# Engine programs in the main block without a closing barrier, and a small input loaded behind ScalarE's table load

## The chip, the cores and the metric

The kernel runs on one core of one Trainium2 chip. The metric is the device time of one execution in microseconds (us), and 2% (4.3 us) is what counts as faster or slower. There is also the *span* of a profiled execution: the time from its first to its last instruction in the trace. The time is longer than the span, and the difference, "time minus span" below, holds what the runtime does around the kernel and the trace does not show. Engines are called PE (TensorE), DVE (VectorE), ACT (ScalarE), POOL (GpSimd) and SP (SyncE); an added q, as in SPq, is that engine's sequencer.

## The reference, cut to what matters

```python
xn = _layernorm(A_x)                                   # A_x: (4, 1, 576)
out = A_x + A(xn, k_cache, v_cache, wq, wo) + B(xn, w1, w2, w3, w4)
# A: q = xn @ wq; attention over the last 2048 cached positions, 16 KV heads, batch 4; @ wo
# B: layernorm, gelu(@ w1), shifted, @ w2, add, layernorm, gelu(@ w3) @ w4, add
```

One token per batch entry: hardly any arithmetic and 88.5 MB of weights and cache to read. The input x has 4.5 KB.

## The kernel before

A helper collects each engine's operations in a list, sorts it by a key, resolves the waits to semaphore counts and emits the list as that engine's program. SP issues nearly all transfers, in one long queue. The parts that the change touches:

```python
# x on ACT's queue, first thing; the large wq load heads SP's queue
ev_x = add_dma([(x_sb[:], x2)], "x", (), -100, engine="act")
ev_wq = [add_dma([(kt_t[:], A_wq[0:512, :].rearrange("(p r) n -> p (r n)", r=4))], "wq", (), -60), ...]
...
# the end: two copies out of PSUM, two stores, each engine waits for its own store to land
for h, eng in ((0, "sp"), (1, "act")):
    ev_o[h] = add_dma([(o2[:, HALF * h:HALF * (h + 1)], out_sb[32 * h:32 * h + B, ...])], ("out", h),
                      [f"fin{h}"], 10000, engine=eng)
    add(eng, lambda e: None, [ev_o[h]], None, 10001)
...
# five programs in a Block: each engine jumps to its own block, then to a common end block
with nc.Block() as block:
    @block.sync
    def _(e):
        emit_program("sp", e)
    ...                                    # gpsimd, vector, scalar, tensor alike
```

When the `Block` is left, every engine branches to an end block in which a barrier stands: each of the four other engines drains and reports to POOL, POOL waits for the four reports and releases all. An equal barrier, which the program's constructor puts there, opens the kernel; the change leaves that one alone.

Of the kernel before, what the change touches and what calls it, by code (L numbers as in the profile page):

```python
# [8 lines left out]
ACTF = mybir.ActivationFunctionType  # L9
# [26 lines left out]
def bass_parallel_sum__sliding_block_cached__mixer_s_mlp__decode_kernel(  # L36
    nc, A_x, A_k_cache, A_v_cache, A_wq, A_wo, B_x, B_w1, B_w2, B_w3, B_w4, out
):
    B, Sq, D = A_x.shape
    _, Hkv, Sk, Dh = A_k_cache.shape  # L40
    Hq = A_wq.shape[1] // Dh
    F = B_w3.shape[1]
# [14 lines left out]
    x2 = A_x.rearrange("b s d -> (b s) d")  # L57
    o2 = out.rearrange("b s d -> (b s) d")

    with ExitStack() as ctx:  # L60
        def sb(name, shape, dt):
            return ctx.enter_context(nc.sbuf_tensor(name, shape, dt))

        def sem(name):
            return ctx.enter_context(nc.semaphore(name))
# [26 lines left out]
        x_sb = sb("x_sb", [B, D], BF16)  # L92
# [18 lines left out]
        act_dummy = sb("act_dummy", [1, 2], BF16)  # L111
# [9 lines left out]
        zeros_bf = sb("zeros_bf", [128, 512], BF16)  # L121
# [35 lines left out]
        def add(engine, emit, waits=(), sig=None, key=0.0, inc=(), loop=None, cond=None):  # L157
            seqc[0] += 1
            prog[engine].append(Op(emit, waits, sig, key, seqc[0], inc, loop, cond))

        def tok(nm):
            if nm not in S:
                S[nm] = sem("t_" + "_".join(str(k) for k in (nm if isinstance(nm, tuple) else (nm,))))
            return nm
# [6 lines left out]
        def add_dma(pairs, skey, waits=(), key=0.0, engine="sp"):  # L171
            tok(skey)
            dma_count[skey] = dma_count.get(skey, 0) + 16 * len(pairs)

            def emit(e):
                for o_, i_ in pairs:
                    e.dma_start(o_, i_).then_inc(S[skey], 16)  # L177
            add(engine, emit, waits, None, key)
            return ("dma", skey, dma_count[skey])
# [11 lines left out]
        def pool_ident(t, tag, pattern, view, key):  # L191
# [19 lines left out]
            waits=["ident_f"], sig="mU", key=-8)  # L211
# [1 line left out]
            add("dve", lambda e, x=x: e.tensor_copy(out=mU_bf[:, :, x], in_=mU[:]), waits=["mU"], sig=f"mU_bf{x}", key=-7.8)  # L213


        ev_x = add_dma([(x_sb[:], x2)], "x", (), -100, engine="act")
        ev_wq = [add_dma([(kt_t[:], A_wq[0:512, :].rearrange("(p r) n -> p (r n)", r=4))], "wq", (), -60),
                 add_dma([(wqrag, rag_src(A_wq))], "wqr", (), -59)]
        ev_w2 = add_dma([(w2main, B_w2[0:512, :].rearrange("(p r) n -> p r n", r=4)), (w2rag, rag_src(B_w2))], "w2", (), -58)
# [98 lines left out]
        for b in range(B):  # L318
            add("dve", lambda e, b=b: e.tensor_copy(out=qp_out[:, b], in_=qp_in[:, b]), waits=["qTp", "qpad_zero"],
                sig="qT" if b == B - 1 else None, key=-29.4)  # L320
# [3 lines left out]
        def pe_zero(e):  # L324
# [2 lines left out]
                ins = e.matmul(Sps[:, q, :], lhsT=zeros_bf[:, 0:128], rhs=zeros_bf[:, :], start=True, stop=True)  # L327
            return ins
        add("pe", pe_zero, waits=["zeros_bf", "perm_bf", "gelu_h", "x1", "xnT"], sig=None, key=-7.5)
        add("act", lambda e: e.activation(out=act_dummy[:], in_=zeros_bf[0:1, 0:2], func=ACTF.Copy), waits=["zeros_bf"], inc=[(tok("evA"), 1)], key=-0.5)  # L330
        add("dve", lambda e: e.tensor_copy(out=dve_dummy[:], in_=zeros_bf[0:1, 0:2]), waits=["zeros_bf"], inc=[(tok("evD"), 1)], key=-0.5)

# [29 lines left out]
        for c in range(NC):  # L362
            lp = ("K", c // NPOS)
            for k in range(NBLK):
# [6 lines left out]
                    key=NBLK * c + k + 0.2)  # L371
# [4 lines left out]
              waits=["qT", "qs_zero"] + ([f"SC{c - NPOS}"] if c >= NPOS - 1 else []), inc=[("qs", 1)], key=c)  # L376
# [6 lines left out]
            waits=["rmax"], sig="negb", key=KS + 0.05)  # L383
        for q in range(4):
            add("act", lambda e, q=q: e.activation(out=P_sb[:, q, :], in_=Sps[:, q, :], func=ACTF.Exp,
                                                   bias=negb[:, 0:1], scale=scale, accum_out=rs4[:, q:q + 1]),
                waits=["negb"], sig=f"exp{q}", key=KS + 0.1 + 0.01 * q)

        for q in range(4):
# [3 lines left out]
                waits=[f"PTx{q}", "permT_bf"] + (["PT0"] if q == 3 else []), sig=f"PTy{q}", key=k0)  # L393
            add("act", lambda e, q=q: e.activation(out=PT_t[:, 512 * q:512 * (q + 1)], in_=ps[:, 4 + q % 3, :], func=ACTF.Copy),
                waits=[f"PTy{q}"], sig=f"PT{q}", key=k0 + 0.16)
# [3 lines left out]
            waits=["rinv", "ident_f"], sig="diag", key=KS + 0.82)  # L399
        add("pe", lambda e: e.matmul(rinvps, lhsT=ones_f[:], rhs=diag[:], start=True, stop=True), waits=["diag", "ones_f", "exp3"],  # L400
            sig="rinvp", key=KS + 0.9)
        add("dve", lambda e: e.tensor_copy(out=rinvB[:].rearrange("p (c u e) -> p c u e", u=NU, e=2),
                                           in_=rinvps.rearrange("p (u c e) -> p c u e", u=NU, e=2)),
            waits=["rinvp"], sig="rinvB", key=KS + 1.5)
# [20 lines left out]
        for c in range(NC):  # L425
# [4 lines left out]
                key=KV + 2 * c, loop=("V", gq))  # L430
            if b == B - 1:
                hv = lambda t, gq=gq: t[:, 0:128].rearrange("p (b h) -> p b h", b=B)[:, :, 8 * gq:8 * gq + 8]
                add("dve", lambda e, hv=hv: e.tensor_tensor(out=hv(OTn), in0=OTps.rearrange("p (b h) -> p b h", b=B), in1=hv(rinvB), op=ALU.mult),  # L433
                    waits=["rinvB", f"PV{c}"], sig=f"OTn{gq}" if gq == 3 else None, inc=[(tok("otn"), 1)] if gq < 3 else [], key=KV + 2 * c + 0.1)
# [13 lines left out]
        def pe_AO(half):  # L448
# [10 lines left out]
            waits=["OTy"], sig="ORp", key=KT - 2.5)  # L459
# [30 lines left out]
        for h in range(2):  # L490
# [3 lines left out]
                waits=[f"hs{h}", "ln1"], sig="x1" if h else "x1a", key=-29 + 0.6 * h)  # L494
# [4 lines left out]
        for h in range(2):  # L499
            add("act", lambda e, h=h: e.activation(out=h_sb[:, HALF * h:HALF * (h + 1)], in_=HTps[h], func=ACTF.Gelu_apprx_tanh),  # L500
                waits=[f"hT{h}", "x1nT"], sig="gelu_h" if h else None, key=-20 + 0.1 * h)
# [29 lines left out]
        for k in range(3):  # L531
            add("act", lambda e, k=k: e.activation(out=h2g[:, 384 * k:384 * (k + 1)], in_=H2ps[k], func=ACTF.Gelu_apprx_tanh), waits=["h2_3"],
                sig="gelu2" if k == 2 else None, key=-0.9 + 0.1 * k)

        def pe_h2T(e):
# [7 lines left out]
            waits=["h2T"], inc=[("evA", 1)], key=-0.3)  # L543
        add("dve", lambda e: e.tensor_copy(out=h2o[:, :, 8, :], in_=H2Tb.rearrange("p (g y) -> p g y", g=4)[..., 0:B]),  # L544
            waits=["h2T"], inc=[("evD", 1)], key=-0.3)
# [35 lines left out]
        def emit_op(eng_name, engine, op, waited):  # L581
            for w in op.waits:
                if isinstance(w, tuple) and w[0] == "take":
                    engine.wait_ge(S[w[1]], w[2]).then_inc(S[w[1]], -w[2])  # L584
                    continue
                s_, v_ = resolve(w)
                if waited.get(s_.num, 0) >= v_:
                    continue
                waited[s_.num] = v_
                engine.wait_ge(s_, v_)  # L590
            ins = op.emit(engine)
            if op.sig is not None:
                ins.then_inc(S[eng_name], 1)
            for nm, n in op.inc:
                ins.then_inc(S[nm], n)

        def emit_program(eng_name, engine):
            waited = {}
            ops = prog[eng_name]
            if eng_name == "pe":  # L600
                hop = engine.alloc_register("hop")
                engine.reg_mov(hop, 0)
            i = 0
            while i < len(ops):
                if ops[i].loop is None:
                    emit_op(eng_name, engine, ops[i], waited)
                    i += 1
                    continue
                name = ops[i].loop[0]
                passes = {}  # L610
                while i < len(ops) and ops[i].loop is not None and ops[i].loop[0] == name:
                    passes.setdefault(ops[i].loop[1], []).append(ops[i])
                    i += 1
                shape = [[(op.sig is None, [w[1:] for w in op.waits], op.inc) for op in p] for p in passes.values()]
                assert all(x == shape[0] for x in shape) and list(passes) == list(range(len(passes)))
                assert all(w[0] == "take" for p in passes.values() for op in p for w in op.waits)
                with engine.bass.Fori(0, len(passes), engines=OrderedEngineSet([engine.engine]), head_slot={engine.engine: 0}):
                    inner = nc.cur_bb
                    for k, op in enumerate(passes[0]):
                        emit_op(eng_name, engine, op, waited)  # L620
                        if (name, k) in HOPS:
                            engine.br_eq(hop, 0, on_true=f"hop_{name}", on_false=f"fall_{name}")
                            nc.switch_bb(f"fall_{name}", parent=inner)
                            engine.sem_inc(S["hop"], 1)
                            engine.br(f"hop_{name}")
                            nc.switch_bb(f"hop_{name}", parent=inner)

        with nc.Block() as block:
            @block.sync
            def _(e):  # L630
                emit_program("sp", e)

            @block.gpsimd
            def _(e):
                emit_program("pool", e)

            @block.vector
            def _(e):
                emit_program("dve", e)

            @block.scalar
            def _(e):
                emit_program("act", e)

            @block.tensor
            def _(e):
                emit_program("pe", e)


# [26 lines left out]
```

## Time and profile before

| | before |
|---|---|
| time, median of 3 runs (range) | 215.94 us (215.93 to 216.82) |
| span of the profiled execution | 214.09 us |
| time minus span, same execution | 1.81 us |
| packets of weights and cache: first starts, last ends | 1.85 us, 211.10 us |

From the page of the kernel before: the busy share of the 16 DMA engines in 40 equal slices of the span, in tenths, and SP's queue with packets, MB and share of 16 engines' span.

```profile
DMA  7999999999999999999999999999999999999992
...
q1 hardware_dynamic: 7432, 88.50, 97.7%
```

The transfers never pause, so they are the bound; only what lies before the first and after the last packet can be saved. The chain of waits of the kernel before, its last pieces (start us, us, what):

```profile
179.19 31.22 DMA w<-in_B_w_dram
210.41 0.04 issue
210.46 1.39 PE ps L438 x18
211.85 0.44 DVE out_sb L560
```

The head, from the timeline of the kernel before (start us, us, engine line operation, out<-in, count, and in brackets the idle time in front and what ended it):

```profile
0.81 0.42 SPq L177 DMA_DIRECT2D kt<-in_A_wq_dram  x1
0.82 0.56 ACTq L177 DMA_DIRECT2D x_sb<-in_A_x_dram  x1
1.41 1.28 ACT L264 ACT_TABLE_LOAD   x1 [1.41 <-PEq L661]
2.26 0.45 DVE L259 BATCH_NORM_STATS2 stats<-x_sb 4x6 f32<-4x288 bf16 x1 [2.26 <-DMA x_sb<-in_A_x_dram]
...
8.51 0.19 PE L281 MATMUL ps<-ident_bf,ragsrc 4*128 4x4 bf16 x2
13.05 3.60 PE L301 MATMUL ps<-kt,xnT 128*32 128x512 bf16 x32 [4.35 <-DMA kt<-in_A_wq_dram]
```

x lands early, the layer norms and their small transposes are through at 8.7 us, and PE then waits for wq until 13.05 us. The end, from the timeline and, for the sequencers, from the view of the source line of the Block's end (engine, operation, count, duration in ns min/median/max, start of the first and of the last):

```profile
212.30 0.28 ACTq L177 DMA_DIRECT2D out_dram<-out_sb  x1
212.31 0.35 SPq L177 DMA_DIRECT2D out_dram<-out_sb  x1
```

```profile
L628 POOLq EVENT_SEMAPHORE  x2: 17/17/17, 213.9 to 214.0; - x2
L628 POOLq DRAIN  x1: 379/379/379, 98.3 to 98.3; - x1
...
L628 SPq COMPARE_BRANCH  x1: 33/33/33, 213.7 to 213.7; - x1
L628 SPq DRAIN  x1: 13/13/13, 213.9 to 213.9; - x1
...
L628 PEldq EVENT_SEMAPHORE  x1: 51/51/51, 214.0 to 214.0; - x1
```

SP knows at 213.70 us that its store has landed, and 0.39 us later the barrier has released the last engine. And POOL was through with its work before 99 us (its drain starts at 98.3) and stands in the barrier until the end: its two semaphore instructions there run from 213.9 us on, and the second ends at 214.00 us.

### The profile page before, as it was taken

Reading aid. Unit: us, or ns where it says so; the run is one execution under the profiler, and the core shown is the slowest. Engines: PE = TensorE matmul, PEld = TensorE weight load, DVE = VectorE, ACT = ScalarE, POOL = GpSimd, SP = SyncE. Lnnn points to the kernel's source line nnn. Section 1 sums busy time; section 2 is a strip of 40 time slices with the busy share of each in tenths; the row PEclk is TensorE's granted clock in tenths of the full one; section 3 lists DMA queues with packets and bytes.
Section 4 is the critical chain, followed back from the end, with each engine's and each line's share of the span. In section 5 each row is a group of like instructions: output and inputs, shape, how many; then the busy total and the mean of one; then the engine's idle time right before and its main releaser. Section 6 shows DMA issues by size and latency. Waiting matters only on the chain. (4 is left out here: it accounts for less than half of the span.)

```text
span 214.1 us, 5906 instructions
## 1 busy us (share of the span) xinstructions
PE 145.6 (68%) x2642; PEld 108.9 (51%) x2646; DVE 76.5 (36%) x150; ACT 61.0 (29%) x75; POOL 10.9 (5%) x37
## 2 busy tenths in 40 slices
PE   0157787999999999999996178033444333336995
PEld 0023312888878887888774068033434333334542
DVE  5305400577676676666664830100010011001000
ACT  2001402466655665666666620000000000000000
POOL 8301000000001000000000000000000000000000
PEclk9999699999999999999999655555555555555799
DMA  7999999999999999999999999999999999999992
GB/s 282 404 385 445 441 407 438 419 427 416 435 429 429 422 435 429 424 426 435 429 426 426 429 429 425 419 432 429 429 422 429 435 429 419 430 436 426 428 409 104
DMA packets 7459, 88.66 MB, mean 414 GB/s; under 512 B 1292, under 2 KB 1688, under 8 KB 2456
## 3 DMA queue, kind: packets, MB, share of 16 engines
q1 hardware_dynamic: 7432, 88.50, 97.7%
q8 instruction: 8, 0.13, 0.2%
q14 instruction: 3, 0.02, 0.0%
q10 hardware_dynamic: 16, 0.01, 0.0%
HBM read 88.49 MB, written 0.00 MB: 413 GB/s over the span
## 5 line engine op out<-in xcount | busy, mean ns | idle before, releaser
L340 PE MATMUL ps<-perm_bf,ring 128*128 128x128 bf16 x1024 | 61.7, 220 | 0.6
L340 PEld LDWEIGHTS ps<-perm_bf,ring 128*128 128x128 bf16 x1024 | 57.5, 98 | 8.9 <-issue 8.6
L347 DVE COPY kt<-ps 128x1024 bf16<-128x1024 bf16 x80 | 52.3, 687 | 24.8 <-PE ps L340 24.3
L421 PE MATMUL ps<-PTpad,ring 128*128 128x8 bf16 x1024 | 29.7, 168 | 41.2 <-PEq L584 37.7
L346 ACT ACTIVATE kt<-ps 128x1024 bf16<-128x1024 bf16 x48 | 48.5, 1023 | 29.1 <-PE ps L340 28.3
L421 PEld LDWEIGHTS ps<-PTpad,ring 128*128 128x128 bf16 x1024 | 28.7, 104 | 42.3 <-issue 42.2
L561 ACT ACTIVATE out_sb<-ps 4x288 bf16<-4x288 f32 x1 | 0.4, 401 | 87.2 <-PE ps L438 87.2
L354 PE MATMUL ps<-kt,Qs 128*32 128x512 bf16 x272 | 17.8, 382 | 1.4 <-PEq L584 1.4
L410 DVE TENSOR_TENSOR PTpad<-PT,mU_bf 128x512 bf16<-128x512 bf16 x16 | 6.4, 420 | 29.7 <-PE ps L421 29.7
L433 DVE TENSOR_TENSOR OTn<-ps,rinvB 128x32 bf16<-128x32 f32 x4 | 0.8, 191 | 34.2 <-PE ps L421 34.2
L523 PE MATMUL ps<-w,x1nT 128*32 128x384 bf16 (+2 forms) x65 | 11.3, 766 | 0.8 <-DMA w<-in_B_w_dram 0.5
L354 PEld LDWEIGHTS ps<-kt,Qs 128*32 128x32 bf16 x272 | 5.8, 96 | 6.8 <-issue 1.5
L375 POOL COPY Qs<-Qpad 128x128 bf16<-128x128 bf16 x16 | 4.6, 293 | 87.0 <-PE ps L354 75.0
L301 PE MATMUL ps<-kt,xnT 128*32 128x512 bf16 x32 | 3.6, 631 | 4.3 <-DMA kt<-in_A_wq_dram 4.3
L523 PEld LDWEIGHTS ps<-w,x1nT 128*32 128x32 bf16 x65 | 3.3, 113 | 6.3 <-issue 3.9
L438 PE MATMUL ps<-w,ORT 128*4 128x288 bf16 x64 | 5.8, 357 | 0.4 <-DVE ORT L460 0.4
L278 PE MATMUL ps<-ident_bf,xn_bf 4*128 4x4 bf16 x8 | 0.6, 170 | 8.0 <-DVE ragsrc L271 8.0
L560 DVE CAST out_sb<-ps 4x288 bf16<-4x288 f32 x1 | 0.4, 446 | 14.5 <-PE ps L438 14.5
L438 PE MATMUL ps<-w,h2T_sb 128*4 128x288 bf16 x72 | 5.0, 286 | 0.4 <-DMA w<-in_B_w_dram 0.4
L392 PE MATMUL ps<-kt,permT_bf 128*128 128x512 bf16 x3 | 1.8, 608 | 4.9 <-DVE kt L391 4.8
L544 DVE COPY h2T_sb<-ps 128x16 bf16<-128x16 bf16 x1 | 0.2, 166 | 13.6 <-PE ps L538 13.6
L438 PEld LDWEIGHTS ps<-w,ORT 128*4 128x4 bf16 x64 | 3.3, 106 | 3.1 <-DVE ORT L460 1.0
(99 smaller groups left out, 61.6 us busy)
## 6 DMA issues: line engine op xcount, KB each, us to landing
ring<-in_A_k_cache_dram SPq DMA_DIRECT2D x32, 1024.0 KB, 13.0
ring<-in_A_v_cache_dram SPq DMA_DIRECT2D x32, 1024.0 KB, 15.1
w<-in_B_w_dram SPq DMA_DIRECT2D x2, 2304.0 KB, 22.9
w<-in_A_wo_dram SPq DMA_DIRECT2D x2, 2304.0 KB, 20.3
kt<-in_A_wq_dram SPq DMA_DIRECT2D x1, 4096.0 KB, 12.2
w<-in_B_w_dram SPq DMA_DIRECT2D x1, 2592.0 KB, 27.4
w<-in_B_w_dram SPq DMA_DIRECT2D x3, 576.0 KB, 14.5
w<-in_B_w_dram SPq DMA_DIRECT2D x1, 1296.0 KB, 30.0
```

Source lines behind the costliest of these rows:

```text
L301: ins = e.matmul(Qps[k][32 * g:32 * g + 32, :], lhsT=x_, rhs=w, start=(r == 0), stop=(r == 4), tile_position=(0, 32 * g), skip_group_check ...
L340: ins = e.transpose(tb[n % 4][:, t, :], slot_t(c)[:, 8 * k + t, :], perm_bf[:])
L346: return "act", lambda e: e.activation(out=ktbuf[:, n % 16], in_=tb[n % 4], func=ACTF.Copy)
L347: return "dve", lambda e: e.tensor_copy(out=ktbuf[:, n % 16], in_=tb[n % 4])
L354: ins = e.matmul(Sps[32 * u:32 * u + 32, q, :].rearrange("p (t i) -> p t i", t=16), lhsT=Qs[:, c % NPOS, 32 * u:32 * u + 32], rhs=ktgrp[:, ...
L375: P(lambda e, c=c, cc=cc: e.tensor_copy(out=Qs[:, c % NPOS, :], in_=Qpad_t[:, 128 * cc:128 * cc + 128]), waits=["qT", "qs_zero"] + ([f"SC{ ...
L392: add("pe", lambda e, q=q: e.matmul(ps[:, 4 + q % 3, :], lhsT=permT_bf[:], rhs=PTx[:, q, :], start=True, stop=True), waits=[f"PTx{q}", "pe ...
L410: return lambda e: e.tensor_tensor(out=PTpad[:, c % 2], in0=PTv[:, :, cc, :].unsqueeze(2).to_broadcast([128, NT, NU, 2]), in1=mU_bf[:].uns ...
L421: ins = e.matmul(o_, lhsT=slot_t(c)[:, t, :], rhs=PTpad[:, c % 2, t].rearrange("p u e -> p (u e)"), start=(t == 0), stop=(t == NT - 1))
L433: add("dve", lambda e, hv=hv: e.tensor_tensor(out=hv(OTn), in0=OTps.rearrange("p (b h) -> p b h", b=B), in1=hv(rinvB), op=ALU.mult), waits ...
L438: return e.matmul(ACC[h], lhsT=lhsT, rhs=rhs, start=start, stop=stop, tile_position=(0, 32 * h), skip_group_check=True)
L523: ins = e.matmul(H2ps[k][32 * g:32 * g + 32, 128 * off:128 * (off + cnt)].rearrange("p (c x) -> p c x", c=cnt), lhsT=x_, rhs=w.rearrange(" ...
```

## The change

Its intent: drop the jumps and the closing barrier, which order nothing that the stores' own waits do not, and keep x's small transfer away from the start of the large one. The diff, cut:

```diff
-        ev_x = add_dma([(x_sb[:], x2)], "x", (), -100, engine="act")
+        ev_x = add_dma([(x_sb[:], x2)], "x", ["sqrt_table"], -100, engine="act")
...
+        add("act", lambda e: e.activation(out=act_dummy[:], in_=zeros_bf[0:1, 0:2], func=ACTF.Sqrt), waits=["zeros_bf"], sig="sqrt_table", key=-110)
...
-        with nc.Block() as block:
-            @block.sync
-            def _(e):
-                emit_program("sp", e)
...      (gpsimd, vector, scalar and tensor alike)
+        for eng_name, engine in (("sp", nc.sync), ("pool", nc.gpsimd), ("dve", nc.vector), ("act", nc.scalar), ("pe", nc.tensor)):
+            emit_program(eng_name, engine)
```

More of the change, by code (lines that the diff above doesn't have):

```diff
@@ L626, in emit_program @@
                             nc.switch_bb(f"hop_{name}", parent=inner)
-        with nc.Block() as block:
-            @block.sync
-            def _(e):
-                emit_program("sp", e)
-            @block.gpsimd
-            def _(e):
-                emit_program("pool", e)
-            @block.vector
-            def _(e):
-                emit_program("dve", e)
-            @block.scalar
-            def _(e):
-                emit_program("act", e)
-            @block.tensor
-            def _(e):
-                emit_program("pe", e)
+        for eng_name, engine in (("sp", nc.sync), ("pool", nc.gpsimd), ("dve", nc.vector), ("act", nc.scalar), ("pe", nc.tensor)):
+            emit_program(eng_name, engine)
 _INS = ['A_x', 'A_k_cache', 'A_v_cache', 'A_wq', 'A_wo', 'B_x', 'B_w1', 'B_w2', 'B_w3', 'B_w4']
```

## The prediction

> **What bounds the kernel now.** The transfers. The line of slices shows DMA at 9 tenths or more in 38 of 40 slices; the SyncE queue takes 97.7% of 16 engines' span (88.5 MB). The chain of waits ends with 31.2 us of weight transfer (landing at 210.4 us), 1.39 us of matmuls and 0.44 us of copy. Only two stretches can give time: the one before the stream of packets and the one after it.
>
> Head (timeline, packets): the opening barrier releases the engines at 0.73 us; the large wq load is issued at 0.810 (0.42 us) and x on ScalarE's queue at 0.817 (0.56 us, against 0.28 for its output store: it seems to wait for the descriptor generator). First packets start at 1.76 (x) and 1.85 us (wq, 1.04 after its issue; the output stores show 0.75 and 0.85). Tail: stores are issued at 212.30; ScalarE sees its store landed at 213.52, SyncE at 213.70; then branch, drain and the five-engine barrier end the span at 214.09.
>
> **What the change does.**
> 1. End barrier and branches go: after SyncE's wait (213.70) some 0.02 us should remain instead of 0.39. Worth 0.35 us, all critical, if what the runtime runs afterwards doesn't grow by as much.
> 2. One branch less per engine at the head, where barrier to first issue is 0.07 us: worth 0.02 to 0.05.
> 3. x moves behind the Sqrt table load (1283 ns in the trace, the figure of the Trainium skill, "ScalarE: Activation LUTs", section "What ACT_TABLE_LOAD costs"). The load now starts at about 0.76 instead of 1.41, then one 0.2 us activation, then x is issued near 2.3 us instead of 0.82. The wq issue is alone, so its packets may start up to 0.2 us sooner; I count 0.1. The price: x now meets wq packets of 32 KB, which took 1.2 to 2.0 us each. The Trainium skill ("DMA: Bandwidth & Descriptors", section "Queues, rings and completion order") says each engine alternates between rows packet by packet, so x should wait for one or two packets and land at 4.5 to 6 us (estimate); DVE's first statistics move from 2.26 to about 5.
>    The layer norms are a chain of 6.4 us from there to the last small transposes (2.26 to 8.70). They would end near 11.5 us, before wq lands at 13.05, for which PE waits 4.4 us today. So it costs nothing; the slack is 4.35 us.
>
> **Sum.** 0.35 + 0.03 + 0.1, about 0.5 us of 215.94: 215.45 us, range 214.9 to 215.95. Runs of before spread from 215.93 to 216.82. Chances: faster by over 2% 0.01, within 2% 0.98, slower by over 2% 0.01.
>
> **What would show the steps.** Right: no drain or barrier after SyncE's last wait, span shorter by 0.4 to 0.6 us; table load at 0.76 us; first wq packets before 1.8 us; DVE's first statistics at 4.5 to 6 us; first q matmul still released by wq, at about 12.9 us; DMA line unchanged in the middle. Wrong: span shorter but the time not (the closing work of the runtime absorbs it); q matmuls released by DVE; wq packets no earlier.
>
> **What would make it wrong.** x landing beyond 6.6 us, which would hold up q (though PE has room behind the ring of four slots); PE's loops stalling on instruction fetches because its stream shifts; engines that end at different times being costlier for what runs after; run-to-run spread of 0.9 us hiding everything.

## The result, and the profile after

| | before | changed |
|---|---|---|
| time, median (range), 6 runs each | 216.02 us (215.91 to 217.14) | 215.18 us (214.94 to 215.36) |
| ratio of the fast runs | | 0.9947, 95% interval 0.9924 to 0.9971 |
| span of the profiled execution | 214.09 us | 213.69 us |
| time minus span, same execution | 1.81 us | 1.25 us |
| packets: first starts, last ends | 1.85, 211.10 us | 1.84, 211.09 us |

A ratio is the mean time of one kernel's fast runs over that of the other's in the same rounds, so not quite the ratio of the medians. Here they differ: two of the six runs of before were about 1 us late (216.82 and 217.14) and weigh in the mean. By the medians the gain is 0.84 us, by the ratio 1.15 us (216.02 x 0.0053). In two repetitions of the changed kernel, reported below, the ratios were 0.9959 and 0.9963, 0.9 and 0.8 us; I take 0.85 us as the size. It counts as "within 2%".

The lines that answer to those shown of before. The page of the changed kernel:

```profile
DMA  7999999999999999999999999999999999999993
...
q1 hardware_dynamic: 7432, 88.50, 97.9%
```

The end of its chain of waits:

```profile
179.21 31.20 DMA w<-in_B_w_dram
210.42 0.04 issue
210.46 1.36 PE ps L439 x18
211.82 0.44 DVE out_sb L561
```

The stretch in the middle did not move at all: the last wait for weights ends at 210.41 in one and 210.42 us in the other. The head, from the timeline of the changed kernel:

```profile
0.81 0.42 SPq L177 DMA_DIRECT2D kt<-in_A_wq_dram  x1
0.81 1.28 ACT L330 ACT_TABLE_LOAD   x1 [0.81 <-PEq L644]
...
2.34 0.56 ACTq L177 DMA_DIRECT2D x_sb<-in_A_x_dram  x1
8.30 0.45 DVE L259 BATCH_NORM_STATS2 stats<-x_sb 4x6 f32<-4x288 bf16 x1 [8.30 <-DMA x_sb<-in_A_x_dram]
...
13.57 0.19 PE L281 MATMUL ps<-ident_bf,ragsrc 4*128 4x4 bf16 x2
13.69 3.60 PE L301 MATMUL ps<-kt,xnT 128*32 128x512 bf16 x32
```

SP's first issue stands at 0.81 us as before, so the missing branch gained nothing. x landed only at 8.3 us, and the matmuls of q start at 13.69 us, straight behind the transposes: q is now released by the layer norms, no longer by wq, and comes 0.64 us later. The tail, from the view of the line that emits waits, in the window from 213 to 214 us:

```profile
L591 ACTq EVENT_SEMAPHORE  x1: 17/17/17, 213.5 to 213.5; - x1
L591 SPq EVENT_SEMAPHORE  x1: 17/17/17, 213.7 to 213.7; - x1
```

SP's wait at 213.67 us is the last instruction. POOL's last instruction is now a copy that ends at 99.69 us; the view of the line of these copies:

```profile
L376 POOL COPY Qs<-Qpad x16: 289/293/294, 20.1 to 99.4; 128x128 bf16<-128x128 bf16 x16
```

So the span lost its 0.40 us as forecast. But the time of the same execution lost 0.96 us: another 0.56 us went from outside the span, where I had expected nothing. That is what the experiments had to explain.

**Theory A.** After its last instruction each engine has closing work of the runtime to do. An engine that ends early does it while the stores are still under way; the barrier made all five end together, and so put the longest piece of that work behind the last instruction. **Theory B.** The barrier's instructions, or the jump to an end block, themselves delay what follows. **Theory C.** The new order of x at the head gains more than I forecast.

The Trainium skill ("Runtime: NRT & Kernel Launch", section "The ~15µs preamble/postamble breakdown") tells of a closing sequence that the runtime appends, with about 1.5 us each for a barrier and for resetting each engine's semaphores. Nothing in these traces shows those instructions, so no run here confirms that this is what the closing work is; only its length, as time minus span, is measured. Those two stages alone would make 3 us, and 1.25 and 1.81 us are measured here, so the measured time can't hold both in full, one after the other, behind the span.

### The profile page after: what moved, and what is told of

It reads as the page before. It is cut to its first block, busy times and chain, and to the rows that moved or that the text cites. A ratio compares the mean times of both kernels' runs of the same rounds, so it can differ in the third digit from the quotient of the medians.

```text
span 213.7 us, 5896 instructions
## 1 busy us (share of the span) xinstructions
PE 145.3 (68%) x2642; PEld 110.1 (52%) x2646; DVE 75.6 (35%) x150; ACT 60.4 (28%) x76; POOL 10.8 (5%) x37
## 5 line engine op out<-in xcount | busy, mean ns | idle before, releaser
L341 PEld LDWEIGHTS ps<-perm_bf,ring 128*128 128x128 bf16 x1024 | 59.0, 99 | 7.3 <-issue 7.0
L347 ACT ACTIVATE kt<-ps 128x1024 bf16<-128x1024 bf16 x48 | 47.7, 1023 | 29.9 <-PE ps L341 29.9
L439 PE MATMUL ps<-w,ORT 128*4 128x288 bf16 x64 | 4.8, 316 | 0.4 <-DVE ORT L461 0.4
L439 PEld LDWEIGHTS ps<-w,h2T_sb 128*4 128x4 bf16 x72 | 2.9, 84 | 3.8 <-DMA w<-in_B_w_dram 2.8
```

The costliest lines, as they stand in the source:

```text
L341: ins = e.transpose(tb[n % 4][:, t, :], slot_t(c)[:, 8 * k + t, :], perm_bf[:])
L347: return "act", lambda e: e.activation(out=ktbuf[:, n % 16], in_=tb[n % 4], func=ACTF.Copy)
L439: return e.matmul(ACC[h], lhsT=lhsT, rhs=rhs, start=start, stop=stop, tile_position=(0, 32 * h), skip_group_check=True)
```

## The experiments

Kernels of one call ran on the same chip; "before" is the kernel before on that chip, 11 runs per call. Time minus span in the tables is of one profiled execution. In the six runs of the changed kernel the difference was 1.24 to 1.36 us, so 0.1 us between two single executions means little; the means over all runs of a kernel stand under "The sum of it".

### Call 1: the halves of the change, and the end taken apart

**e1_x_only.** The block and barrier stay; x waits for the table load.

```diff
 (on the kernel before)
+ ev_x = add_dma([(x_sb[:], x2)], "x", ["sqrt_table"], -100, engine="act")     # and the Sqrt activation
```

> Only the x half of the change: x behind the table load, blocks and end barrier kept. Theory (the end barrier is all of it): time as before within 0.1 us, span 214.1, time minus span 1.8 as in the profiled run of before; x lands near 8 us and q is released by the layer norms, at no cost. Rival (the x order gives part of the gain that I mis-sized): 0.3 us or more below before.

**e2_main_only.** No block and no barrier; x first, as before.

```diff
 (on the changed kernel)
+ ev_x = add_dma([(x_sb[:], x2)], "x", (), -100, engine="act")                 # no Sqrt activation in front
```

> Only the other half: programs in the main block, no end barrier, x issued first as before. Theory: the whole gain of 0.8 to 1.1 us, span 213.7, time minus span 1.3. Rival (x order matters): only about half of the gain.

**e3_wait_all.** No barrier, but every engine waits for both stores.

```diff
             emit_program(eng_name, engine)
+            for h in range(2):
+                engine.wait_ge(S[("out", h)], 16)
```

> The changed kernel, but all five engines wait at their end for the landing of both output stores; no barrier, no drain, no branch. Theory A (the gain outside the span comes from engines that run the closing work of the runtime while the last stores are under way): time minus span goes back to 1.7 or 1.8, time 215.6, span 213.7. Theory B (barrier instructions or the jump to an end block themselves make the closing work start late): time minus span stays at 1.3, time 215.2.

**e4_barrier_in_main.** The barrier, without branches to an end block.

```diff
             emit_program(eng_name, engine)
+        nc.all_engine_barrier()
```

> The changed kernel plus one five-engine barrier at its end, without the branches to an end block. Theory A: span 213.95 (barrier 0.25 us), time minus span 1.8, time 215.75, nearly that of before; the branches are the last 0.15 us. Theory B with the jump at fault: time minus span 1.3, time 215.3.

| same chip | lowest | median | ratio (95%) | profiled: time | span | time minus span |
|---|---|---|---|---|---|---|
| before | 215.80 | 216.06 | | | | |
| e1_x_only | 215.82 | 216.24 | 1.0009 (0.999 to 1.0028) | 217.58 | 215.76 | 1.82 |
| e2_main_only | 214.91 | 215.10 | 0.9954 (0.9941 to 0.9966) | 215.20 | 213.86 | 1.34 |
| e3_wait_all | 215.56 | 215.69 | 1.0007 (0.9978 to 1.0037) | 215.56 | 213.77 | 1.79 |
| e4_barrier_in_main | 215.63 | 215.92 | 1.0003 (0.9983 to 1.0022) | 215.93 | 214.12 | 1.81 |

The x half is worth nothing measurable and the other half is the whole gain: theory C falls. In e1 two of six runs were over 1 us late, the profiled one among them. That one lost its time in the stream, whose last packet ends at 212.72 us instead of 211.09. About half of this was lost between 40 and 60 us, where the transfers moved 410 GB/s and the changed kernel has 428, which is some 0.84 us (estimate, 20 us x 18/428); why is not known (these two lines are the stretches view of e1 and of the changed kernel: window, length, busy us and count of PE, PEld, DVE, ACT, POOL, granted clock, DMA share, GB/s).

```profile
40.00:60.00 20.00, 19.20 (x301) 15.96 (x299) 11.96 (x19) 10.30 (x11) 1.17 (x4) 0.92 1.01 410
```

```profile
40.00:60.00 20.00, 20.00 (x328) 16.83 (x327) 13.17 (x21) 11.95 (x12) 1.17 (x4) 0.95 1.01 428
```

Such runs widen the ratios of e1, e3 and e4 so much that I read the lowest run, the median and the profiled execution instead. By these, e3 settles A against B: the view of its added waits shows no barrier, no branch and no drain.

```profile
L632 SPq EVENT_SEMAPHORE  x2: 17/22/28, 213.7 to 213.7; - x2
...
L632 POOLq EVENT_SEMAPHORE  x1: 192/192/192, 213.5 to 213.5; - x1
...
L632 PEldq EVENT_SEMAPHORE  x1: 192/192/192, 213.5 to 213.5; - x1
```

Its span is that of the changed kernel within 0.1 us, and yet time minus span is back at 1.79 us (1.67 to 1.80 in its six runs, against 1.24 to 1.36 in the changed kernel's). Ending late is enough, and a barrier on top of it adds nothing outside the span (1.70 to 1.83 in the six runs of e4). e4 adds the barrier proper: from SP's wait satisfied (213.84) to the end (214.12) 0.28 us, against 0.39 us with branches and 0.02 us with neither. In medians: before to e4 0.14 us (branches; estimate 0.11 from the spans), e4 to e3 0.23 us (barrier), e3 to e2 0.59 us (late ends).

### Call 2: which engine's end costs

The three edits are one, with another engine's name; e8 moves ACT's wait to SP.

```diff
             emit_program(eng_name, engine)
+            if eng_name == "pe":          # e6: "dve", e7: "pool"
+                for h in range(2):
+                    engine.wait_ge(S[("out", h)], 16)
```

```diff
-            add(eng, lambda e: None, [ev_o[h]], None, 10001)
+        add("sp", lambda e: None, [ev_o[1], ev_o[0]], None, 10001)      # e8; e9: "act" in place of "sp"
```

**e5_pe_waits:**

> The changed kernel, but TensorE too waits at its end for the landing of both stores (ScalarE and SyncE wait as they do in the changed kernel). Waiting of all five cost 0.5 us outside the span (1.76 against 1.30). If each engine has closing work of its own and the longest decides, one of the three engines brings back all of it and the others nothing; I guess TensorE: time 215.6, time minus span 1.75. If the closing work is one chain through the engines, each of the three gives a part, or the first of the chain all.

**e6_dve_waits:**

> The same with VectorE waiting in place of TensorE. Longest-engine theory: nothing, time 215.15 and time minus span 1.3, if TensorE is the long one. Chain theory: a part of the 0.5 us.

**e7_pool_waits:**

> The same with GpSimd waiting in place of TensorE. Longest-engine theory: nothing, time 215.15 and time minus span 1.3, if TensorE is the long one. Chain theory: a part of the 0.5 us.

**e8_sp_waits_alone:**

> The changed kernel, but SyncE alone waits for both stores; ScalarE ends after it has issued its own. Longest-engine theory with ScalarE or SyncE equally short: as the changed kernel, 215.15. If ScalarE's closing work decides the 1.3 us that are left: 0.1 to 0.5 us less, since it ends 1.2 us earlier; that would beat both kernels.

| same chip | lowest | median | ratio (95%) | profiled: time | span | time minus span |
|---|---|---|---|---|---|---|
| before | 215.96 | 216.16 | | | | |
| e5_pe_waits | 215.25 | 215.83 | 0.9994 (0.9969 to 1.002) | 215.58 | 213.98 | 1.60 |
| e6_dve_waits | 215.24 | 215.56 | 0.9982 (0.9963 to 1.0001) | 215.48 | 214.04 | 1.44 |
| e7_pool_waits | 215.62 | 215.75 | 0.9995 (0.9971 to 1.0018) | 215.76 | 213.89 | 1.87 |
| e8_sp_waits_alone | 215.25 | 215.47 | 0.9994 (0.9963 to 1.0024) | 215.33 | 214.08 | 1.25 |

My guess of PE was wrong: it is POOL, whose late end alone brings back the whole 0.5 us; PE brings back part of it, and DVE is hardly outside the scatter. ACT's early end in e8 gained nothing that these runs can show. The medians are blurred by late runs (three of six in e5, two in e6 and in e8), so the verdict rests on the profiled executions and, for POOL, on the lowest run too.

### Call 3: the last engine, the hidden lead, and x

**e9_act_waits_alone** (the edit of e8, with "act"):

> The changed kernel, but ScalarE alone waits for both stores; SyncE ends after it has issued its own. So far, time minus span with the last engine being GpSimd 1.86, TensorE 1.58, VectorE 1.48, SyncE 1.23 to 1.36. If ScalarE's closing work is shorter than SyncE's, time minus span is below 1.2 and this beats the changed kernel by 0.1 us or more; if longer, between 1.3 and 1.45 and it is slower by up to 0.15 us.

**e10_changed_again** is the changed kernel, unedited.

> The changed kernel itself, unaltered, on this chip. The changed kernel and the one with main block only had no run over 215.4 us in 11, all others about one in four some 0.9 us or more above their lowest. If that was chance, one to three of six runs here lie 0.9 us or more above the lowest; if ending unevenly really prevents such runs, none does. Lowest run 215.0 to 215.2, time minus span 1.3.

**e11_small_wq_packets**, one look only:

```diff
-        ev_wq = [add_dma([(kt_t[:], A_wq[0:512, :].rearrange("(p r) n -> p (r n)", r=4))], "wq", (), -60),
+        wq_src = A_wq[0:512, :].rearrange("(p r) n -> p r n", r=4)
+        ev_wq = [add_dma([(wqmain[:, r, :], wq_src[:, r, :]) for r in range(4)], "wq", (), -60),
```

> The changed kernel, but wq comes in four transfers with rows of 8 KB instead of one with rows of 32 KB, so packets a quarter as long. If x waits for a number of packets on its engines (three before its data, one more before its semaphore), its packets start near 4 us instead of 6.2 to 6.7 and VectorE starts near 4.5 instead of 8.3 us. If it waits for all bytes queued ahead of it, nothing changes: 8 us. The time stays within the spread of runs either way.

**e12_pool_ends_at_copy:**

```diff
             emit_program(eng_name, engine)
+            if eng_name == "pool":
+                engine.wait_ge(S["dve"], ev_val["fin0"][1])
```

> The changed kernel, but GpSimd waits at its end for VectorE's last copy (about 212.26 us), 1.4 us before the stores have landed. If only lateness beyond the landing costs (closing work of 1.86 us hidden behind the stores), it would end near 214.15 plus a little, before SyncE's 215.0: time and time minus span as the changed kernel, 1.3. If the mere fact that GpSimd ends in a wait near the end costs (its closing instructions not fetched, or not yet run), time minus span goes to 1.8.

| same chip | lowest | median | ratio (95%) | profiled: time | span | time minus span |
|---|---|---|---|---|---|---|
| before | 215.93 | 216.04 | | | | |
| e9_act_waits_alone | 215.20 | 215.89 | 0.9994 (0.9967 to 1.0021) | 215.27 | 213.78 | 1.49 |
| e10_changed_again | 215.05 | 215.16 | 0.9959 (0.9943 to 0.9975) | 215.10 | 213.85 | 1.25 |
| e11_small_wq_packets | 215.64 (one run) | | | 215.64 | 214.26 | 1.38 |
| e12_pool_ends_at_copy | 215.03 | 215.28 | 0.9972 (0.9953 to 0.9991) | 215.03 | 213.68 | 1.35 |

In e9 time minus span was 1.49 us, near the expected 1.3 to 1.45 for a ScalarE that takes longer than SyncE; its median and ratio are blurred by three late runs of six, and its lowest run lies 0.15 us over that of e10. The added wait of e12 and, for comparison, that of e7, each from the view of its line:

```profile
L632 POOLq EVENT_SEMAPHORE  x1: 17/17/17, 212.3 to 212.3; - x1
```

```profile
L633 POOLq EVENT_SEMAPHORE  x1: 192/192/192, 213.7 to 213.7; - x1
```

POOL ends 113 us later than in the changed kernel (212.31 against 99.69), 1.4 us before the stores have landed, and it costs nothing; 1.6 us later still, in e7, it costs 0.5 us. So it is not that POOL waits, but that it is late. Nor is it the kind of wait, a store's semaphore in e7 and an engine's in e12: in the kernel before and in e4 POOL waits in the barrier for other engines, not for a store, and pays the same when it ends at 214.0 us.

In e11 the timeline shows x issued at the same time and DVE starting 0.9 us sooner than in the changed kernel (the thirteen executions in which x waits behind rows of 32 KB have DVE's start at 8.02 to 9.27 us):

```profile
2.34 0.56 ACTq L177 DMA_DIRECT2D x_sb<-in_A_x_dram  x1
7.40 0.45 DVE L260 BATCH_NORM_STATS2 stats<-x_sb 4x6 f32<-4x288 bf16 x1 [7.40 <-DMA x_sb<-in_A_x_dram]
```

The records of single packets say where: x's data start at 5.80 to 6.57 us, against 6.20 to 6.68 us with rows of 32 KB, but its semaphore writes follow 0.35 us after the data instead of 1.25 us (which all thirteen show). A packet of wq that starts before 9 us takes 0.33 us on average in e11 and 1.34 us in the changed kernel. So the second half of the expectation holds (one more packet before the semaphore), and the first fell: the wait before the data hardly depends on the packet length, so it is no fixed number of packets, and it is far less than all that was queued (1.0 MB had been moved by then, of 4.2 MB of wq). When x's first data start, 1.57 MB of transfers have started in the changed kernel and 1.42 MB in e11, so a fixed time and a fixed amount of data fit alike. What sets it stays open.

### Call 4: one store instead of two

What was open was whether the time follows the last end, and the late runs.

```diff
-        for h, eng in ((0, "sp"), (1, "act")):                 # two stores, two waits
+        ev_o = add_dma([(o2, out_sb[0:B, :])], ("out", 0), ["fin0", "fin1"], 10000)
+        add("sp", lambda e: None, [ev_o], None, 10001)
...
-  out=out_sb[32:32 + B, HALF:D], in_=ACC[1]
+  out=out_sb[0:B, HALF:D], in_=ACC[1]
```

**e13_single_store:**

> The changed kernel with one output store instead of two: ScalarE's copy writes to the same four partitions as VectorE's, and SyncE alone issues the store, after both copies. In the changed kernel SyncE's store takes 0.35 us to issue, 0.07 more than ScalarE's beside it, and is seen landed 0.18 us later. If the time is SyncE's end plus 1.25 us, the span falls by 0.1 to 0.15 us and the time with it: 215.0 where the changed kernel shows 215.1 to 215.2 on this chip. If something else than the last end decides, the span falls and the time doesn't.

**e14_changed_third** is the changed kernel, unedited.

> The changed kernel unaltered, beside the single store on the same chip: 215.1 to 215.2 median, time minus span 1.25. Of its 12 runs so far one lay 0.8 us above its lowest, against about three in ten of the others; if that is chance, one or two of these six lie 0.8 us or more above the lowest.

| same chip | lowest | median | ratio (95%) | profiled: time | span | time minus span |
|---|---|---|---|---|---|---|
| before | 215.84 | 215.99 | | | | |
| e13_single_store | 214.89 | 215.12 | 0.9967 (0.9949 to 0.9985) | 215.10 | 213.78 | 1.32 |
| e14_changed_third | 215.09 | 215.19 | 0.9963 (0.9950 to 0.9976) | 215.09 | 213.75 | 1.34 |

The single store beats nothing. From DVE's last copy to SP's end it takes 1.40 us where e14 takes 1.43. My reason had a flaw that this run shows: SP's store takes 0.35 us to issue when it is alone too, so it had not been waiting for ACT's.

The late runs: the changed kernel had one run of 17 that lay 0.7 us or more above its lowest of the same call, the kernel before 4 of 50. That is no difference; the other variants, some that end early among them (e8 and e12, two of six each), had more, and I have no explanation for them.

### The sum of it

Call the *lead* of an engine the time that must still pass after its last instruction. Five runs, one per engine, give the five leads as their time minus that engine's end (the end that I take to decide): GpSimd 1.87 (e7), TensorE 1.60 (e5), ScalarE 1.49 (e9), VectorE 1.44 (e6), SyncE 1.25 us (e8). Whatever part of the measured time lies before the first instruction of the trace is contained in a lead too; no trace shows it. All runs of these kernels, with spans to 0.1 us, give means of time minus span that agree within 0.06 us:

| kernel | what ends last | runs | time minus span, range | mean |
|---|---|---|---|---|
| e7_pool_waits | GpSimd with SyncE | 6 | 1.82 to 1.92 | 1.86 |
| e5_pe_waits | TensorE with SyncE | 6 | 1.49 to 1.67 | 1.57 |
| e9_act_waits_alone | ScalarE alone | 6 | 1.36 to 1.51 | 1.45 |
| e6_dve_waits | VectorE with SyncE | 6 | 1.32 to 1.48 | 1.44 |
| e8_sp_waits_alone | SyncE alone | 6 | 1.21 to 1.37 | 1.31 |
| changed (first call) | SyncE, ScalarE 0.18 us sooner | 6 | 1.24 to 1.36 | 1.32 |

By their means GpSimd and TensorE stand clear of the rest; ScalarE and VectorE can't be told apart, and both lie about 0.1 us over SyncE. The time should then be the largest of end plus lead over the five engines. Nine of the other eleven profiled executions test that:

| execution | engine that decides | its end | plus lead | measured time |
|---|---|---|---|---|
| before | GpSimd (in the barrier) | 214.00 | 215.87 | 215.90 |
| changed | ScalarE (SyncE 0.06 less) | 213.51 | 215.00 | 214.94 |
| e1 | GpSimd (in the barrier) | 215.67 | 217.54 | 217.58 |
| e2 | ScalarE | 213.68 | 215.17 | 215.20 |
| e3 | GpSimd | 213.68 | 215.55 | 215.56 |
| e4 | GpSimd (in the barrier) | 214.03 | 215.90 | 215.93 |
| e10 | ScalarE | 213.67 | 215.16 | 215.10 |
| e12 | ScalarE (GpSimd: 212.31 + 1.87 = 214.18) | 213.50 | 214.99 | 215.03 |
| e13 | SyncE | 213.78 | 215.03 | 215.10 |

All nine agree within 0.07 us (so do e11 and e14, with 0.07 and 0.03). Two limits: the test bears on GpSimd, and on ScalarE and SyncE as a pair, but no execution here is decided by TensorE or VectorE, so their leads rest on e5 and e6 alone; and where the table names ScalarE, SyncE lies within 0.1 us, so which of the two decides is not shown (by the means it would be SyncE in the changed kernel). The rule needs no view of the closing work itself. It does not tell whether each engine has a piece of its own of that length or whether the engines pass a token along a chain; both give this maximum.

## Why the prediction was right or wrong, point by point

- **The bound, and "within 2%": right.** The stream runs from 1.84 to 211.09 us in the changed kernel and from 1.85 to 211.10 before; the time of 215.18 us lies in the stated range. That is luck in part: the range was wide enough for 0.56 us of which no term of the sum spoke.
- **Size: wrong.** About 0.5 us was forecast; the medians gave 0.84 and the ratio 1.15 us, the repetitions 0.8 to 0.9.
- **The step that failed: "Worth 0.35 us, all critical, if what the runtime runs afterwards doesn't grow by as much."** The span lost what was said: 0.39 us after SP's wait became 0.02. But I allowed the work after the span to grow or stay, not to shrink. It shrank from 1.81 to 1.25 us, since the barrier had made GpSimd, idle since 99 us and with the longest lead, end with the others. The term should have been about 0.9 us: 215.87 to 215.00 us by the rule above. I looked at the last instruction of the chain instead of at every engine's last instruction.
- **Step 2, one branch less at the head, 0.02 to 0.05 us: not there.** SP's first issue stands at 0.81 us in both.
- **Step 3, wq's packets 0.1 us sooner: not there.** 1.84 against 1.85 us, and e1 shows no gain. So x's issue had not been holding up SP's first one. ACT's issue of x takes 0.56 us at 2.34 us as it did at 0.82; since SP issues other loads at that time too (1.74 to 5.32 us), what makes it so long stays open.
- **Step 3, x lands at 4.5 to 6 us: wrong,** 7.9 us by its last semaphore write and 8.3 for DVE. I counted one or two packets; x's data waited 3.3 us after the end of its issue (2.90 to 6.20), and then one more packet of 1.25 us stood before the semaphore. The skill's page "DMA: Bandwidth & Descriptors", section "Queues, rings and completion order", says that an engine alternates between rows packet by packet, but counts about 9 to 17 descriptors as a typical packet. I took one packet of the trace for one of these, which no run here shows. Taken so, the semaphore's delay fits the page, and the first wait, longer than one packet, does not.
- **"So it costs nothing; the slack is 4.35 us": the time was right, the slack was used up.** x came 6.0 us later (8.30 against 2.26), q 0.64 us later. The slack did not suffice; that the time held all the same fits the room that I had named as the second reserve, the ring. The lines for it stand below this list.
- **"Wrong: ... the closing work of the runtime absorbs it":** the closing work was named as a risk with the wrong sign, and so were "engines that end at different times being costlier for what runs after": here they were cheaper.

From the page of the kernel before and of the changed one, the transfers of K into the ring (KB each, median us from issue to landing):

```profile
ring<-in_A_k_cache_dram SPq DMA_DIRECT2D x32, 1024.0 KB, 13.0
```

```profile
ring<-in_A_k_cache_dram SPq DMA_DIRECT2D x32, 1024.0 KB, 11.0
```

The K loads land 11 to 13 us after their issue, so SP issues them that far ahead. In the changed kernel SP waits longer for PE to free slots of the ring (88.3 us in 16 waits against 84.8), and the loads spend 2 us less in the queue. Not all of that is the work of x: e2, with x first, shows 87.6 us of waits and 11.8 us to landing. That a late q costs nothing is seen more plainly in e12, where x lands later still: q starts at 14.62 us, 1.57 us later than before, and the last packet of weights ends at 211.08 us, against 211.10 before.

## What to carry to other kernels

At the end of a kernel, look at every engine's last instruction and not only at the chain that ends last: what the runtime does afterwards behaves as if it started engine by engine, and an engine with nothing left to do should be let go, not kept in a barrier. Where the stores' own waits already make the results safe, a closing barrier costs more than its instructions (0.3 us of span here, 0.5 us beyond it). And a change whose effect lies partly outside the span must be judged by the time, with time minus span taken from the same execution.

## What the Trainium skill lacked or had wrong

- "Runtime: NRT & Kernel Launch", section "The ~15µs preamble/postamble breakdown": it gives one length for each closing stage, but not that the time left after an engine's last instruction differs by engine (1.87 us with GpSimd last, 1.60 TensorE, 1.49 ScalarE, 1.44 VectorE, 1.25 SyncE, one execution each; means over six runs above) and that an engine that ends early hides it.
- "DMA: Bandwidth & Descriptors", section "Queues, rings and completion order": the packet-by-packet alternation, with its packets of about 9 to 17 descriptors, does not tell how long a small load waits behind a large one that is already running: 3.3 us after its issue ended with packets of 32 KB, 2.9 us with packets of 8 KB, and then one packet more (1.25 or 0.35 us) before its semaphore.
- "ScalarE: Activation LUTs", section "What ACT_TABLE_LOAD costs": the 1283 ns are in every trace here; the drain of about 1380 ns beside it is not: in the changed kernel the load ends at 2.094 us and the Sqrt activation starts at 2.106. So it is at the switch to another table set at 24.30 us: the load ends at 25.583 and the next activation starts at 25.595 us.
- No page that I read gives the time that a store of a few KB takes to issue by engine: 0.28 us on ScalarE, and 0.35 us on SyncE, beside ScalarE's or alone (e13); the load of x, 4.5 KB on ScalarE, took 0.56 us.
